# Queries and keys of five batches come in through DRAM rows and transposing DMAs in place of VectorE block transposes (sparse attention feeding a bilinear feed-forward layer)

## The chip, the cores and the metric

The kernel runs on one core of a Trainium2 chip. The core has a matrix engine (TensorE, PE in the profile, with its weight loads shown as PEld), VectorE (DVE), ScalarE (ACT), GpSimd (POOL) and a queue engine SyncE (SP), and 16 DMA engines that serve all queues. The metric is the device time of one execution in microseconds (us). Three runs of the kernel before took 330.50, 330.77 and 330.81 us; their median is 330.77.

## The reference

Eight batches of eight heads, 576 tokens, head width 64, all inputs float32. Heads 0 to 3 attend to the 32 latest tokens (local); heads 4 to 7 to earlier tokens with the same position modulo 32 (strided). The heads' outputs, side by side, are the 4608 x 512 input of a bilinear layer:

```python
scores = scale * np.matmul(q, k.transpose(0, 1, 3, 2))
mask_local = (rel >= 0) & (rel < stride)                      # stride = 32
mask_strided = (rel >= 0) & (pos[None, :] % stride == pos[:, None] % stride)
scores = np.where(masks[None], scores, -1e9)                  # heads 0-3 local, 4-7 strided
attn = softmax(scores);  x = (attn @ v) as rows of 512
return (x @ w_a) * (x @ w_b) @ w_out                          # 512 -> 1536 -> 512
```

## The kernel before, in words

**Stages.** Batch 0's attention runs by itself. After it the feed-forward layer runs over nine tiles of 512 tokens, and the attention of batches 1 to 7 is cut into small steps that are put between its matmuls. A tile has 16 slots: 12 `ffn_ab` (L627; eight 512-wide matmuls give both projections of 128 hidden units, ScalarE copies one out of PSUM, VectorE multiplies it with the other into `pf`) and 4 output slots (`ffn_y` L874 for tiles 0 and 1, `ffn_ys` L862 for tiles 2 to 8, which works with sums `ps` of pieces of `pf`, made by `fast_s` L753). Tiles 7 and 8 (`JOINT`) use the same kind of sums for the first projections: `wsum` of the weights (L656, L661) and `xsum` of the activations. Batch b's attention runs beside tile b-1, and tile b needs it.

**The order is written out by hand.** Every engine runs its instructions in program order. `do(i, fn, ...)` (L997) hangs a function behind slot i, where slot 16 t is the first of tile t; `LATER` (L587) and `IN_Y` (L590) place the attention steps of batches 3 to 7, counted from slot 16 (b-1): S0 to S7 are score units (`S_p` L379: matmuls; `S_x`: exponential on ScalarE; `S_m` L415: mask by a bitwise AND on VectorE), V0 to V7 value units, O0 and O1 store finished rows to DRAM (`rows_out` L505), I0 and I1 bring them back transposed into `xT` (`rows_in` L512). Two units make up one pair of heads, each with half of the pair's blocks. Before a slot's list is run, POOL copies one element of that slot's result (`pace`, L1060), so the DMAs that POOL issues follow the slots; SP has no such copy and goes on as soon as what its next DMA needs is there.

**q and k.** Scores need them with the head width on the partitions: `kT` for k, and for q a pair of buffers `qz` with zeros in the half that belongs to the other head of a pair, so that both heads of a pair go through one matmul. Batches 0 and 1 are transposed on PE. From batch 2 (`FIRST_D`) POOL's queue loads them, cast to bf16, into `kl`, `ql` (local, L213) and `natk`, `natq` (strided, L204), one DMA for each head. VectorE transposes 32x32 blocks (`step_D` L321; L328 four times and L333 six times for a batch), and SP copies the blocks to `kT` and `qz` (L343, L347), 24 copies a batch. There are two sets of buffers, for even and odd batches. `rezero` (L352) writes the zeros of one set on POOL at slot 14.

**Value units.** `step_VT` (L516), used for strided heads from batch 2, makes the value product with the head width on the partitions and the row sums beside it, takes 1/sum on ScalarE (Ln L536, Exp L537), and multiplies the two heads of a unit in two VectorE instructions into `xT` (L543).

**Weight sums.** `wsum_make` runs at slots 98 to 105, in tile 6: sums of `w_a` on VectorE, those of `w_b` on POOL, eight instructions each (L666).

Of the kernel before, what the change touches and what calls it, by code (L numbers as in the profile page):

```python
# [10 lines left out]
ALU = mybir.AluOpType  # L11
# [20 lines left out]
def kernel(  # L32
# [230 lines left out]

    held = {}
# [56 lines left out]
    def step_D(b, z, nm, part):  # L321
# [15 lines left out]
        if last:  # L337
            for nm, c in {"k": (("k", 0),), "q": (("q", 0), ("k", 1), ("q", 1))}[nm]:
# [10 lines left out]
                if (nm, c, z) == ("q", 0, 0) and b - 1 > FIRST_D:  # L349
                    rows_in(b - 1, 1)  # L350

    def rezero(b):  # L352

        for j in range(2):
            for t in qz_buf[b % 2][j]:
                nc.gpsimd.memset(t[32:64] if j == 0 else t[64:96], 0.0)
# [22 lines left out]
    def S_p(b, u):  # L379
# [136 lines left out]
    def step_VT(b, u):  # L516
# [70 lines left out]
    LATER = {-1: "S0", 0: "S1", 1: "V0", 2: "S2", 3: "V1 O0", 4: "S3", 5: "V2", 6: "S4 I0", 7: "V3 O1", 8: "S5", 9: "V4",  # L587
# [39 lines left out]
    def ffn_ab(t, f, mid, ab=None):  # L627
# [28 lines left out]
    wsum = [[h.rearrange("p (c g m) -> p c g m", c=2, g=FG) for h in homes] for homes in (  # L656
        [flat(vl_buf[0])[:, WS * z:WS * (z + 1)] for z in range(2)] + [flat(t)[:, :WS] for t in qz_pair[0]],
        [flat(vs_all[0])[:, WS * z:WS * (z + 1)] for z in range(2)] + [flat(nat_s[nm]) for nm in "qk"])]
    xsum = {t: flat(qz_pair[1][t - 7])[:, :8 * HT].rearrange("p (n c m) -> p n c m", n=4, c=2) for t in JOINT}

    def wsum_make(s, n, eng):  # L661
        w, s_ = (lambda e, j: wviews[s][:, j, :, :, e]), wsum[s]
        a, b, op = ((w(1, 0), w(1, 1), ALU.add), (s_[0], w(0, 0), ALU.subtract), (w(0, 0), w(1, 0), ALU.subtract),
                    (w(0, 1), s_[1], ALU.subtract))[n]
        for c in range(2):
            eng.tensor_tensor(s_[n][:, c], a[:, c], b[:, c], op=op)  # L666
# [33 lines left out]
    def joint(t):  # L700
# [3 lines left out]
        for half, (plain, *gs) in enumerate(JOINT[t]):  # L704
            banks = {x: eight(x) for x in "Ya Yb Xb Zb Xa Za".split()}
            order = JOINT_ORDER[half].split()
            for at_, (k, m) in enumerate(order):
# [10 lines left out]
                else:  # L718
# [190 lines left out]
    with tc.manual_schedule(engines={ENG.PE, ENG.SP, ENG.Pool, ENG.DVE, ENG.Activation}):  # L909
# [83 lines left out]
        steps[16 * (B - 2) + 9][-1][1].append("I1")  # L993
# [15 lines left out]
        for b in range(FIRST_D, B):  # L1009
# [13 lines left out]
            gs = {2: (14, 14, 15, 15, 16, 16, 17, 17, 18, 18), 3: (8, 9, 10, 11, 12, 13, 14, 15, 16, 17)}.get(b) or (  # L1023
                3, 5, 7, 9, 12, 13, 14, 15, 16, 17)
# [69 lines left out]
```

## Time and profile before

The profile is of one execution.

| | |
|---|---|
| median of three runs | 330.77 us (330.50 to 330.81) |
| the profiled execution | 331.63 us, its span 329.9 us |
| granted TensorE clock | 1.00 |
| busy share of the span | PE 96%, DVE 81%, ACT 57%, POOL 55% |
| block transposes on DVE from batch 2 on | L328 24 times (765 ns), L333 36 times (704 ns) |
| DVE multiply into xT (L543) | 48 times, 445 ns |
| weight sums (L666) | DVE 8 times, 543 to 553 ns; POOL 8 times, 1627 to 1952 ns |
| loads of q and k on POOL's queue, batches 2 to 7 | 96 DMAs, 72 or 96 KB each |
| copies to kT and qz on SP's queue | 144 DMAs |
| transposing DMAs xT from xd | 11, median 4.5 us from issue to landing |

The page's first part gives each engine's busy time, the second the span in 40 slices with the busy share in tenths. A line of a group or of a wait names the line of the kernel, the engine, and the tiles as output<-input. A window gives, for a stretch of the span, the busy time of each engine, and at its end the granted clock, the DMA share and GB/s. PE's matmuls are pipelined, so their listed lengths overlap.

### The profile page before, as it was taken

To read this page: it belongs to the slowest core of one execution; us is meant where nothing else is said; L and a number is where in the kernel's file an instruction comes from. 1 tells how busy PE (TensorE), PEld (TensorE's weight loads), DVE (VectorE), ACT (ScalarE), POOL (GpSimd) and SP (SyncE) were. 2 spreads that over 40 slices of the span, in tenths; PEclk is the share of its full clock that TensorE was granted. 3 is DMA by queue.
4 is the path that set the end of the run, shared out by engine and by line. 5 is a ranking of instruction groups with operands and counts; after the bars stand their busy time and mean duration, and the time that the engine had idled before them with its cause. 6 is when DMAs were issued, how large, how long until landed. Compare 5 with 4: busy or idle time off the path is not lost.

```text
span 329.9 us, 7496 instructions
## 1 busy us (share of the span) xinstructions
PE 317.1 (96%) x2691; PEld 212.8 (64%) x2720; DVE 267.3 (81%) x551; ACT 188.7 (57%) x320; POOL 180.2 (55%) x295
## 2 busy tenths in 40 slices
PE   8999999999999999999999999999986799999995
PEld 6754555445555586557999875578543577787775
DVE  7766887888778889889889888988999977864882
ACT  6764764468764575457644764476544555525532
POOL 8845836899857444754475347632278405312350
PEclk9999999999999999999999999999999999999999
DMA  9999999899999999999999999998164013003003
GB/s 158 149 204 201 203 182 168 185 182 130 141 211 130 135 100 92 124 208 121 119 120 215 123 114 107 188 171 103 31 173 59 0 24 108 0 0 129 2 1 127
DMA packets 111920, 40.73 MB, mean 123 GB/s; under 512 B 89868, under 2 KB 108940, under 8 KB 111884
## 3 DMA queue, kind: packets, MB, share of 16 engines
q0 software_dynamic: 85968, 19.48, 64.7%
q1 hardware_dynamic: 25772, 20.71, 26.0%
q8 instruction: 21, 0.34, 0.4%
q14 instruction: 15, 0.12, 0.1%
q10 hardware_dynamic: 144, 0.07, 0.1%
HBM read 39.51 MB, written 11.06 MB: 153 GB/s over the span
## 4 chain that ended last, share of the span: by engine, by line
PE 72%; DMA 8%; DVE 8%; POOL 7%; issue 3%; ACT 1%; POOLq 0%; DVEq 0%
PE mm L624 32%; PE mm L818 13%; PE mm L880 5%; DMA vl<-in_v_dram 4%; DMA shared<-in_q_dram 4%; PE st L389 3%; PE o L527 2%; PE eA L624 2%; PE eXb L728 2%; PE eXa L728 2%; PE eB L624 2%; DVE ps L760 2%; POOL shared L198 2%; PE eYa L818 2%; DVE pf L648 2%
## 5 line engine op out<-in xcount | busy, mean ns | idle before, releaser
L624 PE MATMUL mm<-xT,wb_sb 128*128 128x512 bf16 (+1 forms) x373 | 85.0, 352 | 4.2 <-DVE pf L648 3.9
L624 PE MATMUL mm<-xT,wa_sb 128*128 128x512 bf16 (+1 forms) x360 | 83.9, 351 | 0.7
L645 ACT COPY a_sb<-mm 128x512 f32<-128x512 f32 x82 | 47.9, 585 | 49.0 <-PE mm L624 41.5
L624 PEld LDWEIGHTS <-wb_sb 128*128 128x128 bf16 x416 | 40.1, 98 | 39.9 <-issue 5.2
L624 PEld LDWEIGHTS <-wa_sb 128*128 128x128 bf16 x416 | 37.3, 98 | 22.7 <-DVE xT L543 0.3
L1060 POOL CAST pace<-pf 1x1 f32<-1x1 bf16 x71 | 22.8, 321 | 45.2 <-DVE pf L648 31.8
L648 DVE TENSOR_TENSOR pf<-a_sb,mm 128x512 bf16<-128x512 f32 x60 | 40.7, 679 | 6.4 <-PE mm L624 6.1
L410 ACT ACTIVATE p<-st 72x576 bf16<-72x576 f32 (+1 forms) x56 | 36.4, 650 | 16.2 <-PE st L389 16.0
L543 DVE TENSOR_TENSOR xT<-o,xr 64x288 bf16<-64x288 f32 x48 | 21.4, 445 | 13.5 <-ACT xr L537 13.0
L818 PEld LDWEIGHTS <-ps 128*128 128x128 bf16 x288 | 27.9, 98 | 3.9 <-DVE ps L760 0.7
L732 POOL TENSOR_TENSOR pf<-vl 128x256 bf16<-128x256 f32 x12 | 8.7, 729 | 30.8 <-DVE vl L741 30.8
L536 ACT ACTIVATE xr<-o 64x576 f32<-64x576 f32 x28 | 18.1, 647 | 12.6 <-PE o L527 12.3
L880 PE MATMUL mm<-wo_sb,pf 128*128 128x512 bf16 x93 | 23.2, 379 | 0.2
L818 PEld LDWEIGHTS <-pf 128*128 128x128 bf16 x216 | 20.1, 98 | 3.7 <-DVE pf L648 1.2
L244 POOL DMA_DIRECT2D vs<-in_v_dram x24 | 19.6, 818 | 5.0 <-PE mm L818 2.4
L760 DVE TENSOR_TENSOR ps<-pf 128x512 bf16<-128x512 bf16 (+2 forms) x42 | 21.6, 514 | 0.6
L818 PE MATMUL mm<-wf,ps 128*128 128x256 bf16 x180 | 21.5, 273 | 0.5 <-DVE ps L760 0.5
L537 ACT ACTIVATE xr<-xr 64x576 f32<-64x576 f32 x28 | 19.1, 683 | 0.9
L213 POOL DMA_DIRECT2D ql<-in_q_dram x24 | 15.9, 664 | 6.2 <-DMA wo_sb<-in_moe_w_out_dram 4.6
L213 POOL DMA_DIRECT2D kl<-in_k_dram x24 | 16.1, 671 | 5.3 <-issue 3.2
L791 ACT COPY y_sb<-mm 128x512 f32<-128x512 f32 x20 | 11.7, 585 | 12.1 <-PE mm L818 10.5
L650 DVE TENSOR_TENSOR pf<-a_sb,mm 128x512 bf16<-128x512 f32 x22 | 14.9, 677 | 4.5 <-ACT a_sb L645 2.7
(242 smaller groups left out, 640.0 us busy)
## 6 DMA issues: line engine op xcount, KB each, us to landing
out_dram<-y_sb SPq DMA_DIRECT2D x12, 512.0 KB, 5.5
out_dram<-y_sb SPq DMA_DIRECT2D x11, 256.0 KB, 4.2
vl<-in_v_dram POOLq DMA_DIRECT2D x6, 384.0 KB, 7.7
kl<-in_k_dram POOLq DMA_DIRECT2D x24, 72.0 KB, 3.1
ql<-in_q_dram POOLq DMA_DIRECT2D x24, 72.0 KB, 3.3
vs<-in_v_dram POOLq DMA_DIRECT2D x24, 72.0 KB, 4.2
wo_sb<-in_moe_w_out_dram POOLq DMA_DIRECT2D x4, 384.0 KB, 9.8
natk<-in_k_dram POOLq DMA_DIRECT2D x20, 72.0 KB, 3.5
```

What stands on the lines that cost most here:

```text
L213: nc.gpsimd.dma_start(out=t[32 * h:32 * h + 32], in_=src[b, h].rearrange("(i y) d -> y i d", y=32))
L244: nc.gpsimd.dma_start(out=vs_buf[b % 2][:, h, :, 0:D], in_=v[b, HL + h].rearrange("(p r) d -> p r d", r=RS))
L410: nc.scalar.activation(p_flat(p)[:M, :2 * W].rearrange("p (i n) -> p i n", n=2 * n), st[:M].rearrange("p a (i n) -> p (a i) n", n=256)[:, ...
L537: nc.scalar.activation(r, r, ACT.Exp, scale=-1.0)
L543: nc.vector.tensor_mul(dst.rearrange("d (p r) -> d p r", r=RS)[:, :, G * half:G * (half + 1)], o[:64, j, :W].rearrange("d (g p) -> d p g", ...
L624: nc.tensor.matmul(ps_[:, c0:c0 + n], lhsT=w[:, kk, 128 * f:128 * (f + 1)], rhs=xT[:, kk, x0:x0 + n], start=(kk == first and c0 == 0), sto ...
L645: nc.scalar.copy(a_sb, ab[0])
L648: nc.vector.tensor_mul(pf[:, f, :].rearrange("p (i a s) -> p a i s", i=2, s=16), halves(a_sb), halves(ab[1]))
L760: nc.vector.tensor_tensor(s[:, n], a, b, op=op)
L818: nc.tensor.matmul(bank[b][:, q], lhsT=lhs(g, q), rhs=rhs(g), start=k in "172" and q == 0 and g == 0, stop=g == FG - 1, skip_group_check=True)
L880: nc.tensor.matmul(ybank[j], lhsT=pf[:, f, 128 * j:128 * (j + 1)], rhs=wo_sb[:, f], start=(f == 0), stop=(f == FD - 1))
L1060: nc.gpsimd.tensor_copy(pace, done)
```

## The change

For batches 3 to 7, six DMAs of POOL's queue (`rows_load`, at slots 2 to 7 of tile b-2) read q and k from DRAM in float32 and write them as bf16 rows to DRAM: k and two copies of q for the local heads, and the same for the strided heads. Each copy of q has room for both heads of a pair, and only one head's columns are written; the other columns were filled with zeros once (`rows_zero`, slot 17). Six transposing DMAs of SP's queue (`rows_take`, at slots 5, 6, 7, 9, 10, 11) bring the rows into `kT` and `qz`. The 32x32 transposes, the copies to `kT` and `qz`, and `rezero` go for these batches; batch 2 keeps them. Strided rows hold a head's 8 x 64 values in a row, so a strided unit becomes all 576 tokens of one head instead of half of two heads; `S_p` and `step_VT` have a branch for it, and the multiply into `xT` is one instruction. I1 gets a place of its own at slot 9. All weight sums go to VectorE, one 128x768 instruction at a slot: ten at every third slot of tiles 4 and 5 from slot 65 on, six at every second slot of tile 6 from slot 97 on, with new homes in memory.

```diff
+    def rows_zero(z):
+        rows["q", z] = [dram.tile([(S, NR)[z], (4, 8)[z] * D], BF16, tag=f"zq{z}{j}", name=f"zq{z}{j}", bufs=1) for j in range(2)]
+        rows["k", z] = dram.tile([(S, NR)[z], (4, 8)[z] * D], BF16, tag=f"zk{z}", name=f"zk{z}", bufs=1)
+        for j in range(2):
+            t = rows["q", z][j].rearrange("a b -> (a b)").rearrange("(p n m) -> p n m", p=64, n=2)
+            zero = qz_pair[1][0][64 - 64 * j:128 - 64 * j, j].rearrange("p c n -> p (c n)")
+            nc.sync.dma_start(out=t, in_=zero.unsqueeze(1).to_broadcast([64, 2, 2 * S]))
+
+    def rows_load(b, nm, z, j=0):
+        h0 = b * H + HL * z
+        src = {"k": k, "q": q}[nm].rearrange("b h s d -> (b h) s d")
+        if nm == "k":
+            if z:
+                nc.gpsimd.dma_start(out=rows["k", 1].rearrange("(h p) m -> h p m", h=HL),
+                                    in_=src[h0:h0 + HL].rearrange("h (p r) d -> h p (r d)", r=RS))
+            else:
+                nc.gpsimd.dma_start(out=rows["k", 0].rearrange("s (h d) -> h s d", d=D), in_=src[h0:h0 + HL])
+        elif z:
+            nc.gpsimd.dma_start(
+                out=rows["q", 1][j].rearrange("n (i e d) -> n i e d", e=2, d=D)[:, :, j],
+                in_=src[h0:h0 + HL].rearrange("h (p i e) d -> (h p) i e d", e=2, i=RS // 2)[:, :, j])
+        else:
+            nc.gpsimd.dma_start(out=rows["q", 0][j].rearrange("s (c e d) -> c s e d", e=2, d=D)[:, :, j],
+                                in_=src[h0:h0 + HL].rearrange("(c e) s d -> c s e d", e=2)[:, :, j])
+
+    def flat_s(t):
+        return t[:, :4 * NR].rearrange("p (i m) -> p i m", i=4)
+
+    def rows_take(b, nm, z, j=0):
+        if nm == "k":
+            t = kT_buf[b % 2][z]
+            nc.sync.dma_start_transpose(out=flat_s(t.rearrange("p c n -> p (c n)")) if z else t[:, :, PAD:], in_=rows["k", z])
+        else:
+            t = qz_pair[b % 2][z][:, j]
+            nc.sync.dma_start_transpose(out=flat_s(t.rearrange("p c n -> p (c n)")) if z else t, in_=rows["q", z][j])
...
-                if (nm, c, z) == ("q", 0, 0) and b - 1 > FIRST_D:
-                    rows_in(b - 1, 1)
-
-    def rezero(b):
-
-        for j in range(2):
-            for t in qz_buf[b % 2][j]:
-                nc.gpsimd.memset(t[32:64] if j == 0 else t[64:96], 0.0)
...
+            if b > FIRST_D and c >= 2:
+                kf = kT.rearrange("p c n -> p (c n)")
+                for i in range(G):
+                    k0 = i * NR + (u - HL) * NP
+                    nc.tensor.matmul(sv[:, i, :2 * n].rearrange("p (j n) -> p j n", j=2), lhsT=kf[:, k0:k0 + 128],
+                                     rhs=qz_pair[b % 2][1].rearrange("p j c n -> p j (c n)")[:, :, k0:k0 + n],
+                                     start=True, stop=True)
+                return
...
+        if b > FIRST_D and c >= 2:
+            by_token = lambda x: x[:, :, :W].rearrange("d j (g p) -> d p g j", p=NP)
+            r = r.rearrange("d (p g j) -> d p g j", g=G, j=2)
+            nc.scalar.activation(r, by_token(o[64:]), ACT.Ln)
+            nc.scalar.activation(r, r, ACT.Exp, scale=-1.0)
+            dst = xT[64 * half:64 * half + 64, c, S * (b % XR):S * (b % XR + 1)]
+            nc.vector.tensor_mul(dst.rearrange("d (p g j) -> d p g j", g=G, j=2), by_token(o[:64]), r)
+            return
...
-    LATER = {-1: "S0", 0: "S1", 1: "V0", 2: "S2", 3: "V1 O0", 4: "S3", 5: "V2", 6: "S4 I0", 7: "V3 O1", 8: "S5", 9: "V4",
+    LATER = {-1: "S0", 0: "S1", 1: "V0", 2: "S2", 3: "V1 O0", 4: "S3", 5: "V2", 6: "S4 I0", 7: "V3 O1", 8: "S5", 9: "V4 I1",
...
-    def wsum_make(s, n, eng):
...
-        for c in range(2):
-            eng.tensor_tensor(s_[n][:, c], a[:, c], b[:, c], op=op)
+    def wsum_make(s, n, c):
...
+        nc.vector.tensor_tensor(made(n), a, b, op=op)
...
+                for n, (nm, z, j) in enumerate((("k", 0, 0), ("q", 0, 0), ("q", 0, 1), ("k", 1, 0), ("q", 1, 0), ("q", 1, 1))):
+                    do(g0 + n + 2, rows_load, b, nm, z, j)
+                    do(g0 + n + (5, 5, 5, 6, 6, 6)[n], rows_take, b, nm, z, j)
                 for h in range(HL):
-                    do(g0 + h + (2 if b == FIRST_D + 1 else -2), load_qk, b, False, (h,))
-                    do(g0 + h + (6 if b == FIRST_D + 1 else 2), load_qk, b, True, (h,))
                     do(g0 + h + 10, load_vs, b, (h,))
...
-        for n in range(4):
-            do(16 * (NT - 3) + 2 * n + 2, wsum_make, 0, n, nc.vector)
-            do(16 * (NT - 3) + 2 * n + 3, wsum_make, 1, n, nc.gpsimd)
+        for n in range(16):
+            do(16 * (NT - 5) + 3 * n + 1 if n < 10 else 16 * (NT - 3) + 2 * (n - 10) + 1, wsum_make, n // 8, n // 2 % 4, n % 2)
...
-        do(14, rezero, 1)
         do(28, fill_v, vs_buf[1])
+        do(17, rows_zero, 0)
+        do(17, rows_zero, 1)
```

The sizes are D = 64, S = 576, HL = 4 heads, RS = 8 tokens in a strided row, NR = 288 strided rows, W = 288, NT = 9 tiles. In the text, k0 is the load or take of k for the local heads, q0 even and q0 odd are the two copies of q for them, and k1 and q1 those for the strided heads.

More of the change, by code (lines that the diff above doesn't have):

```diff
@@ L259, in load_wo @@
         )
+    rows = {}
+    NR = HL * S // RS
+    def rows_zero(z):
[30 more added lines that the diff above has]
+            nc.sync.dma_start_transpose(out=flat_s(t.rearrange("p c n -> p (c n)")) if z else t, in_=rows["q", z][j])
     held = {}
@@ L524, in step_VT @@
                     vt = vl_buf[b % 2][:, (2 * c + j) * 6 + 3 * half + i]
+                elif b > FIRST_D:
+                    vt = vs_buf[b % 2][:, u - HL, 2 * i + j]
                 else:
@@ L655, with wsum_home @@
     WS = 2 * FG * 128
-    wsum = [[h.rearrange("p (c g m) -> p c g m", c=2, g=FG) for h in homes] for homes in (
-        [flat(vl_buf[0])[:, WS * z:WS * (z + 1)] for z in range(2)] + [flat(t)[:, :WS] for t in qz_pair[0]],
-        [flat(vs_all[0])[:, WS * z:WS * (z + 1)] for z in range(2)] + [flat(nat_s[nm]) for nm in "qk"])]
-    xsum = {t: flat(qz_pair[1][t - 7])[:, :8 * HT].rearrange("p (n c m) -> p n c m", n=4, c=2) for t in JOINT}
-    def wsum_make(s, n, eng):
-        w, s_ = (lambda e, j: wviews[s][:, j, :, :, e]), wsum[s]
-        a, b, op = ((w(1, 0), w(1, 1), ALU.add), (s_[0], w(0, 0), ALU.subtract), (w(0, 0), w(1, 0), ALU.subtract),
-                    (w(0, 1), s_[1], ALU.subtract))[n]
-        for c in range(2):
-            eng.tensor_tensor(s_[n][:, c], a[:, c], b[:, c], op=op)
+    wsum = {}
+    def wsum_home(i):
+        if i < 3:
+            at_ = ([nat.tile([128, NY, D], BF16, tag=f"{nm}l", name=f"{nm}l") for nm in "kq"] if i == 0 else
+                   [blocks(nm, i - 1) for nm in "kq"])
+            at_ = [flat(t)[:, :WS // 2] for t in at_]
+        else:
+            at_ = (flat(nat_s["kq"[i - 3]]) if i < 5 else flat(vl_buf[0])[:, WS * (i - 5):WS * (i - 4)] if i < 7 else
+                   flat(qz_pair[0][0])[:, :WS])
+            at_ = [at_[:, WS // 2 * c:WS // 2 * (c + 1)] for c in range(2)]
+        return [t.rearrange("p (g m) -> p g m", g=FG) for t in at_]
+    xsum = {t: flat(qz_pair[1][t - 7])[:, :8 * HT].rearrange("p (n c m) -> p n c m", n=4, c=2) for t in JOINT}
+    def wsum_make(s, n, c):
+        if c == 0:
+            wsum[s, n] = wsum_home(4 * s + n)
+        w, made = (lambda e, j: wviews[s][:, j, c, :, e]), (lambda n: wsum[s, n][c])
+        a, b, op = ((lambda: (w(1, 0), w(1, 1), ALU.add)), (lambda: (made(0), w(0, 0), ALU.subtract)),
+                    (lambda: (w(0, 0), w(1, 0), ALU.subtract)), (lambda: (w(0, 1), made(1), ALU.subtract)))[n]()
+        nc.vector.tensor_tensor(made(n), a, b, op=op)
     def x_part(t, j, k):
@@ L725, in joint @@
                         for c in range(2):
-                            w = wsum[s][lhs][:, c, g] if isinstance(lhs, int) else wviews[s][:, lhs[1], c, g, lhs[0]]
+                            w = wsum[s, lhs][c][:, g] if isinstance(lhs, int) else wviews[s][:, lhs[1], c, g, lhs[0]]
                             x = xsum[t][:, rhs, c] if isinstance(rhs, int) else x_part(t, *rhs)[:, c]
@@ L992 @@
                     steps["y", b - 1, n] = [(b, names.split())]
-        steps[16 * (B - 2) + 9][-1][1].append("I1")
         at = {}
@@ L1017 @@
             else:
+                for n, (nm, z, j) in enumerate((("k", 0, 0), ("q", 0, 0), ("q", 0, 1), ("k", 1, 0), ("q", 1, 0), ("q", 1, 1))):
+                    do(g0 + n + 2, rows_load, b, nm, z, j)
+                    do(g0 + n + (5, 5, 5, 6, 6, 6)[n], rows_take, b, nm, z, j)
                 for h in range(HL):
-                    do(g0 + h + (2 if b == FIRST_D + 1 else -2), load_qk, b, False, (h,))
-                    do(g0 + h + (6 if b == FIRST_D + 1 else 2), load_qk, b, True, (h,))
                     do(g0 + h + 10, load_vs, b, (h,))
                 do(g0 + (10 if b == FIRST_D + 1 else 7), load_vl, b)
-            gs = {2: (14, 14, 15, 15, 16, 16, 17, 17, 18, 18), 3: (8, 9, 10, 11, 12, 13, 14, 15, 16, 17)}.get(b) or (
-                3, 5, 7, 9, 12, 13, 14, 15, 16, 17)
+                continue
+            gs = (14, 14, 15, 15, 16, 16, 17, 17, 18, 18)
             for (z, nm, part), g in zip(((0, "k", 0), (0, "k", 1), (0, "q", 0), (0, "q", 1), (1, "k", 0), (1, "k", 1),
```

## The prediction

> **What bounds the kernel now.** I read the page's first two parts first (where is TensorE not full?), then windows of time, then who waited, then the instructions of the one bad stretch.
>
> ```profile
> PE 317.1 (96%) x2691; PEld 212.8 (64%) x2720; DVE 267.3 (81%) x551; ACT 188.7 (57%) x320; POOL 180.2 (55%) x295
> ...
> PE   8999999999999999999999999999986799999995
> ...
> DVE  7766887888778889889889888988999977864882
> ...
> DMA  9999999899999999999999999998164013003003
> ```
>
> TensorE (PE) is full but for the ends and slices 29 to 31. Windows (PE, weight loads, DVE, ACT, POOL busy; clock; DMA share, which passes 1 when one engine has several packets in flight; GB/s):
>
> ```profile
> 80.00:120.00 40.00, 39.74 (x281) 21.83 (x285) 33.18 (x68) 26.22 (x43) 25.48 (x46) 1.00 1.13 142
> 200.00:240.00 40.00, 39.78 (x300) 24.60 (x303) 35.12 (x73) 23.31 (x39) 17.87 (x36) 1.00 0.89 121
> ...
> 240.00:250.00 10.00, 7.99 (x53) 3.92 (x53) 9.93 (x16) 3.74 (x7) 7.35 (x8) 1.00 0.73 152
> 250.00:255.00 5.00, 4.05 (x28) 1.94 (x27) 5.00 (x7) 2.95 (x5) 5.00 (x4) 1.00 0.29 59
> 255.00:260.00 5.00, 3.11 (x31) 2.15 (x31) 4.92 (x8) 2.17 (x4) 4.20 (x5) 1.00 0.00 0
> ```
>
> From 80 to 240 us, where the block transposes stand, the four windows of 40 us leave PE idle 0.26, 0.16, 0.16 and 0.22 us: 0.80 in all. VectorE (DVE) is 83 to 88% busy there and is waited for almost nowhere, so time taken off it there is worth nearly nothing. From 240 to 260 DVE is full (19.85 of 20) and PE loses 4.85. PE's waits name it:
>
> ```profile
> PE mm L624 <- DVE pf L648: 3.9, 4, 1.1
> PE mm L818 <- DVE pf L648: 0.9, 1, 0.9
> ...
> PE mm L818 <- DVE ps L760: 0.5, 1, 0.5
> ```
>
> All of these fall between 244 and 262 us and sum to 5.3 us. What fills DVE there (start, length, instruction), with POOL's timeline below it:
>
> ```profile
> 242.52 0.41 DVE L760 TENSOR_TENSOR ps<-pf 128x512 bf16<-128x512 bf16 x1
> 244.14 1.75 DVE L760 TENSOR_TENSOR ps<-pf 128x512 bf16<-128x512 bf16 x1
> 246.42 1.42 DVE L428 TENSOR_TENSOR p<-p,mask_s 72x576 int16<-72x576 int16 x1
> 259.78 0.44 DVE L428 TENSOR_TENSOR p<-p,mask_s 72x576 int16<-72x576 int16 x1
> ```
>
> ```profile
> 243.80 3.72 POOL L666 TENSOR_TENSOR vs<-vs,wb_sb 128x768 bf16<-128x768 bf16 x2
> 249.98 3.73 POOL L666 TENSOR_TENSOR natq<-wb_sb 128x768 bf16<-128x768 bf16 x2
> ```
>
> The same DVE instruction takes 0.4 us alone and 1.3 to 1.9 beside a weight sum on POOL. Seven are stretched so: L428 1.93, 1.42, 1.43 against 0.45, L760 1.75, 1.75, 1.32, 1.15 against 0.42, 7.7 us in excess. DVE is full because POOL's eight sums collide with it.
>
> **The change, part by part.**
>
> *Weight sums.* All sixteen go to DVE, ten of them 30 to 60 us earlier. POOL's eight (14.1 us) end, and with them the 7.7 us of stretching. DVE still makes six at 0.545 us between 238 and 262, as many as now. Of the 19.85 us in 240 to 260, some 7.5 go with the stretching and 0.5 with the joined products below; 11.9 us stand in the 15 us that the stretch then takes, 80%, under the 88% of 200 to 240 where PE hardly waits. So I take the whole 5.3 us. From below: if half the waits stay, 2.6. The ten early sums (5.5 us) go where DVE loses more than that; without that cover they would lie in the 12 to 17% of DVE time that is idle there.
>
> *Block transposes.* For five batches 4 x 765 ns and 6 x 704 ns go: 7.28 us each, 36.4 in all. By the 0.80 us of idle PE between 80 and 240 this is worth at most that; I take 0.2 us, since only the waits on DVE can shrink. What comes next is PE itself.
>
> *Products of the attention output.* Score and value matmuls keep number and shape. The strided half's two 64x288 multiplies (0.90 us a pair) become one of 64x576: by the fixed part and slope of 64x288 at 445 ns and 128x512 at 679, about 0.75. Twenty units, 3 us on DVE, worth 0. The two ScalarE passes (647 and 683 ns) keep their size and read the banks in another order; if they doubled, ScalarE would go from 58 to some 74% in 200 to 240: still 0.
>
> *POOL's queue.* Per batch eight issues at 0.67 and eight at 0.60 go (10.2 us), six come at 0.6 to 1.36 (the 384 KB load of v is the largest row): at most 8. Zero fills of 4.4 us go. Each issue stands behind a pace copy as now: 0.
>
> *SP's queue.* Per batch 24 copies at about 0.6 us (14.4) go; six transposes come. The 144 KB one of now issues in 1.2 us, so twice the size takes 1.2 to 2.4: 7 to 14. Four zero stores (2.4 us at 0.6) come ahead of batch 2's last qz0s copies: those were issued at 68.5 to 71.0, land 3.1 later and are read at 77.5, so 1.1 us is left. Cost 0; without that margin about 1 us, once.
>
> *DMA traffic.* Rows of these steps:
>
> ```profile
> vl<-in_v_dram POOLq DMA_DIRECT2D x6, 384.0 KB, 7.7
> kl<-in_k_dram POOLq DMA_DIRECT2D x24, 72.0 KB, 3.1
> ...
> xd<-xl SPq DMA_DIRECT2D x10, 144.0 KB, 4.8
> ...
> xT<-xd SPq DMA_TRANSPOSE x11, 4.5
> ```
>
> Per batch there were 4608 pieces of 128 B and 576 of 1 KB; now 6912 and 288. Queue 0's 85,968 packets took 64.7% of 16 engines' 329.9 us, 39.7 ns each: 2016 more pieces cost 5.0 us of all 16 engines. A 144 KB transpose shows a share of 0.68 in a window of 1 us, so six double ones 8.2; the 1024 rows copied now go (26.0% over 25,772 packets is 53 ns, 3.4 us). Net 9.8 us per 33 us tile, 0.3 on a share of 0.9 to 1.4; between 149 and 151 us it reached 2.3 with PE full. Not a limit by itself.
>
> *The new chain of waits.* Load, then transpose, then scores, and SP stands still at each transpose until its load has landed. Behind take k0 waits I0; behind takes q0 wait O1 and I1, whose reader is the next tile's first matmul. In tile 3 of the trace pace copies end slots 2, 3, 4 at 134.3, 136.3, 138.2, which is when the k0, q0 even and q0 odd loads would be issued; S0 needs their transposes at 161.2. At the speed of v's load (3072 pieces in 7.7 us) the three loads' 4608 pieces land 11.6 us after 134.3, and 1.7 later for a DRAM target (xd 4.8 against kl 3.1 for 576 pieces each): 147.6. The last transpose lands by 152 to 155 (4.5 to 7.4, the row's range). Some 6 to 9 us are left, so the cost is 0; this is the value I take, as the same cast of the same 256-byte pieces is the nearest row. The other end is the second rival's.
>
> Sum: 5.3 + 0.2 - 0 = 5.5 us off, of which I leave 0.2 for new small waits: 5.3. The profiled execution took 331.63 (span 329.9 and 1.7 around it) and would take 326.3; the median shown is 0.9 lower, 330.77, so I predict 325.5.
>
> **The rivals.**
>
> *1. Casts to DRAM go out on few engines and land late (slower).* Every load now has 128 or 72 rows of SBUF outermost; k0 has 4 heads outermost and each q0 2 pairs, so the pieces could be split over 4 and 2 DMA engines: 576 in a row on each. At 39.7 ns that is 22.9 us: q0 odd, moving from about 139, lands at 163.6 with the DRAM surcharge, its transpose at 168.1, and PE stands 6.9 us at S0. Five batches make 34 us: 360. In the window 149 to 150 the engines moved 153 GB/s, 9.6 each, or 13.4 ns a piece; then q0 odd lands at 148.4 and nothing waits. It begins to cost at 28 ns (161.2 less 139, 1.7 and 4.5 leaves 16.0 us for 576) and outweighs the 5.3 us at 30. Midway at 33 ns PE waits 3.0 us a batch: 340. For it: no load of the trace has so few outermost rows, and an average piece costs more than 28. Against: packets overlap at the shares above 1. The Trainium skill's page "DMA: Bandwidth & Descriptors", section "Why a DMA increments its semaphore by 16 and not by 1", states this rule: the engine count is the largest number up to 16 dividing both patterns' slowest dimension. By it k0 would run on 4 engines and each q0 on 2, and the sum would be this rival's; no transfer of the trace before shows such a shape.
>
> *2. The waits of 240 to 262 stay.* If DVE is held up there by its own order (mask, product, sum before pf), not by POOL, only the 0.2 and a part of the 5.3 come: 329. For it: six sums remain. Against: 7.7 us of stretching lie exactly beside POOL's sums.
>
> *3. It frees DVE and PE follows.* If PE were really paced by DVE's 83 to 88%, 36 us less would show as more than 5.3. Against: 0.80 us idle in 160. At most 324.7, with the 0.80 all gained.
>
> **How the numbers follow.** Forecast 0.58 (323.5 to 327.5); late casts 0.32, of which 0.26 slower, 0.03 the same, 0.03 still faster; waits stay 0.08 (0.05 faster, 0.01 the same, 0.02 slower); rival 3 0.02. Faster 0.68, the same 0.04, slower 0.28, the bound being 0.2%, about what a measurement of this kernel tells from no change. The range must reach into the late casts: 323.5 to 339 leaves out some 0.15, nearly all above.
>
> **What would show it.** Right: no L666 on POOL, L428 and L760 at 0.4 to 0.5 us throughout, PE over 99% from 240 to 256, no PE wait naming a transpose or xd. Wrong: S0 (L389) or the first matmul of a tile (L624) waiting for kT, qz or xT at each tile's start, SP standing at the transposes for over 10 us, loads landing after 15 us or more.

## The result, and the profile after

The changed kernel takes 465.9 us (median of four runs, 462.51 to 466.99) where the kernel before took 330.79 us beside it: 1.406 times as long (95% interval 1.398 to 1.414). The profiled execution took 466.99 us, its span 465.3. The prediction was 325.5 us, with a range to 339: wrong in sign and far outside. Medians and ratios below leave out runs more than 1.5% above the fastest run of the same kernel (the first experiment has 338.5 us so, and 341.07 over all its runs).

The page's busy shares, some rows of its 40 slices, and its line for POOL's DMA queue (packets, MB, share of 16 engines):

```profile
PE 328.0 (71%) x2691; PEld 217.1 (47%) x2720; DVE 232.1 (50%) x489; ACT 189.7 (41%) x320; POOL 155.4 (33%) x216
...
PE   8999996500999900999007992059950299999996
...
PEclk9999999765899955899757998569985599999999
...
q0 software_dynamic: 208128, 19.94, 62.2%
```

TensorE was full before; from the eighth slice on there is a hole in every tile, with all engines low together, and the granted clock falls there (0.50 from 350 to 365 us, inside the last long hole). No engine took over as the bound. The waits of PE (us in total, times, longest) name the transfers of the change:

```profile
PE st L428 <- DMA qz1l<-zq: 49.7, 2, 24.9
PE st L428 <- DMA qz0l<-zq: 45.9, 2, 24.0
PE o L568 <- DMA vs<-in_v_dram: 13.9, 1, 13.9
PE st L428 <- DMA qz0s<-tq: 9.0, 1, 9.0
PE o L568 <- issue: 8.0, 1, 8.0
```

Four waits of 21.9 to 24.9 us stand at S0 of batches 4 to 7, two at value units (13.9 for v, which comes through the same queue, and 8.0 for which the profile names no releaser), and one of 9.0 us in batch 2. With the small ones (xT 1.8, qz0l from tq 0.7, issue 0.7) that is 129.7 us. Take off the 5.3 us of waits for `pf` and `ps` that are gone, and add 10.9 us by which PE's busy time rose with the same 2691 matmuls (328.0 against 317.1, the lower clock): 135.3, and the spans differ by 135.4.

What happens in one tile is in POOL's timeline (start, length, instruction, and in brackets the idle time before it). L283 is the load of k0, L289 those of q0 even and odd, L280 and L285 those of the strided half:

```profile
136.69 2.98 POOL L283 DMA_DIRECT2D zk<-in_k_dram  x1 [0.76 <-issue]
...
149.62 2.94 POOL L289 DMA_DIRECT2D zq<-in_q_dram  x1 [9.78 <-DVE pf L697]
...
162.40 2.95 POOL L289 DMA_DIRECT2D zq<-in_q_dram  x1 [9.37 <-issue]
...
165.47 0.52 POOL L280 DMA_DIRECT2D zk<-in_k_dram  x1
...
166.10 0.82 POOL L285 DMA_DIRECT2D zq<-in_q_dram  x1
```

and SP's, in the same tile:

```profile
149.26 1.28 SPq L298 DMA_TRANSPOSE kT0l<-zk  x1
150.64 1.22 SPq L553 DMA_TRANSPOSE xT<-xd  x1
162.11 1.30 SPq L301 DMA_TRANSPOSE qz0l<-zq  x1
163.51 0.52 SPq L548 DMA_DIRECT2D xd<-xl  x1
175.39 2.19 SPq L301 DMA_TRANSPOSE qz0l<-zq  x1
```

Three casts go out one after the other, 12.9 and 12.8 us apart, and SP's takes follow each landing: 149.3, 162.1, 175.4. POOL issues the next cast 0.3 to 0.4 us after each take. In the next three tiles the two casts of q0 last as long (12.5 to 13.2 us from issue to take), k0 15.6 to 16.6. The last transpose lands at 184.5, PE having stood at S0 since 162.6. The strided casts and the loads of v come only behind the third cast. The DMA issues show the same (KB each, median us from issue to landing, over the local and the strided casts together); before, `vl` took 7.7 and `vs` 4.2:

```profile
zk<-in_k_dram POOLq DMA_DIRECT2D x10, 288.0 KB, 12.6
zq<-in_q_dram POOLq DMA_DIRECT2D x20, 144.0 KB, 12.6
...
vl<-in_v_dram POOLq DMA_DIRECT2D x6, 384.0 KB, 17.0
vs<-in_v_dram POOLq DMA_DIRECT2D x24, 72.0 KB, 14.4
```

The parts of the change that lie on the compute engines did what was said of them. A window over the tiles that hold the last attention and the early sums, which is free of loads (PE, weight loads, DVE, ACT, POOL busy; clock; DMA share; GB/s), and the joined multiply into `xT`:

```profile
380.00:440.00 60.00, 59.73 (x483) 44.05 (x487) 43.83 (x88) 33.28 (x59) 13.19 (x24) 1.00 0.19 55
```

```profile
L577 DVE TENSOR_TENSOR xT<-o,xr 64x576 bf16<-64x576 f32 x20 | 15.0, 750 | 19.8 <-ACT xr L575 19.6
```

**On how many engines a cast goes out** can be counted. POOL's queue carries 208,128 packets; with the rows put outermost in k0 and q0 (the first experiment, the same data) it carries 92,928. The 115,200 more hold 0.46 MB (19.94 against 19.48), 4 bytes each. They are 5 batches x 576 x (12 + 14 + 14): one packet of 4 bytes for each of the 576 pieces of an engine's row, on every engine that the cast does not use, if k0 is on 4 engines and each q0 on 2. With one q0 alone in the old form (E10) the surplus is 40,320 = 5 x 576 x 14, with both 80,640. The rule of the Trainium skill's page "DMA: Bandwidth & Descriptors", section "Why a DMA increments its semaphore by 16 and not by 1", the largest number up to 16 that divides both sides' slowest dimension, gives 4 and 2, and the trace agrees.

The first experiment also changes the order in which the pieces are written. The trace's records of single packets tell which of the two matters. While q0 even goes out alone (152.6 to 162.1 us), its 1152 packets of 128 bytes take 32.0 ns each, with 3.9 in flight in the mean; from 137 to 145 us of the first experiment such packets take 31.8 ns, with 12 in flight. A packet takes the same time in either order; fewer go at a time.

### The profile page after: what moved, and what is told of

The parts are those of the page before. It is cut to its first block, busy times and chain, and to the rows that moved or that the text cites. A ratio compares the mean times of both kernels' runs of the same rounds, so it can differ in the third digit from the quotient of the medians.

```text
span 465.3 us, 7147 instructions
## 1 busy us (share of the span) xinstructions
PE 328.0 (71%) x2691; PEld 217.1 (47%) x2720; DVE 232.1 (50%) x489; ACT 189.7 (41%) x320; POOL 155.4 (33%) x216
## 3 DMA queue, kind: packets, MB, share of 16 engines
q0 software_dynamic: 208128, 19.94, 62.2%
## 4 chain that ended last, share of the span: by engine, by line
PE 38%; DMA 29%; issue 23%; POOL 6%; SPq 2%; DVE 2%; ACT 0%; POOLq 0%; DVEq 0%
PE mm L673 19%; DMA zq<-in_q_dram 11%; DMA xT<-xd 7%; PE mm L940 3%; DMA vl<-in_v_dram 3%; DMA shared<-in_k_dram 3%; DMA vs<-in_v_dram 2%; PE mm L878 2%; PE eA L673 1%; DMA kT1l<-zk 1%; SPq L301 1%; PE eXb L788 1%; PE eXa L788 1%; PE eB L673 1%; POOL shared L198 1%
## 5 line engine op out<-in xcount | busy, mean ns | idle before, releaser
L289 POOL DMA_DIRECT2D zq<-in_q_dram x10 | 29.4, 2943 | 115.0 <-issue 48.6
L697 DVE TENSOR_TENSOR pf<-a_sb,mm 128x512 bf16<-128x512 f32 x60 | 41.1, 685 | 28.8 <-PE mm L673 15.4
L673 PEld LDWEIGHTS <-wa_sb 128*128 128x128 bf16 x416 | 38.7, 101 | 26.9 <-issue 4.9
L1120 POOL CAST pace<-pf 1x1 f32<-1x1 bf16 x64 | 14.5, 227 | 96.4 <-DVE pf L697 58.6
L428 PE MATMUL st<-qz1l,kT1l 128*128 128x192 bf16 x48 | 7.3, 265 | 49.7 <-DMA qz1l<-zq 49.7
L467 DVE TENSOR_TENSOR p<-p,mask_l 128x576 int16<-128x576 int16 x32 | 14.6, 455 | 52.4 <-ACT p L449 52.2
L428 PE MATMUL st<-qz0l,kT0l 128*128 128x192 bf16 x36 | 5.7, 273 | 46.5 <-DMA qz0l<-zq 45.9
L428 PEld LDWEIGHTS <-kT1l 128*128 128x128 bf16 x48 | 4.7, 104 | 52.7 <-issue 50.7
L428 PEld LDWEIGHTS <-kT0l 128*128 128x128 bf16 x36 | 3.5, 107 | 50.2 <-issue 48.5
L568 PE MATMUL o<-p,vs 72*128 72x72 bf16 x192 | 10.6, 198 | 21.9 <-DMA vs<-in_v_dram 13.9
L244 POOL DMA_DIRECT2D vs<-in_v_dram x24 | 19.9, 831 | 16.4 <-DMA zq<-in_q_dram 13.5
L577 DVE TENSOR_TENSOR xT<-o,xr 64x576 bf16<-64x576 f32 x20 | 15.0, 750 | 19.8 <-ACT xr L575 19.6
L568 PEld LDWEIGHTS <-vs 72*128 72x128 bf16 x192 | 9.5, 99 | 25.4 <-DMA vs<-in_v_dram 14.0
## 6 DMA issues: line engine op xcount, KB each, us to landing
zk<-in_k_dram POOLq DMA_DIRECT2D x10, 288.0 KB, 12.6
zq<-in_q_dram POOLq DMA_DIRECT2D x20, 144.0 KB, 12.6
vs<-in_v_dram POOLq DMA_DIRECT2D x24, 72.0 KB, 14.4
```

Of the source, the lines that this page charges most:

```text
L244: nc.gpsimd.dma_start(out=vs_buf[b % 2][:, h, :, 0:D], in_=v[b, HL + h].rearrange("(p r) d -> p r d", r=RS))
L289: nc.gpsimd.dma_start(out=rows["q", 0][j].rearrange("s (c e d) -> c s e d", e=2, d=D)[:, :, j], in_=src[h0:h0 + HL].rearrange("(c e) s d - ...
L467: nc.vector.tensor_tensor(pi, pi, mk, op=ALU.bitwise_and)
L577: nc.vector.tensor_mul(dst.rearrange("d (p g j) -> d p g j", g=G, j=2), by_token(o[:64]), r)
L673: nc.tensor.matmul(ps_[:, c0:c0 + n], lhsT=w[:, kk, 128 * f:128 * (f + 1)], rhs=xT[:, kk, x0:x0 + n], start=(kk == first and c0 == 0), sto ...
L697: nc.vector.tensor_mul(pf[:, f, :].rearrange("p (i a s) -> p a i s", i=2, s=16), halves(a_sb), halves(ab[1]))
```

## The experiments

The theory after the result: the three casts of the local half go out on few engines, last 12.6 us and more each and one after another, and all that stands behind them on POOL and SP is late. Rivals: the transposes and the added traffic would cost as much with any shape; or the time is lost only because the casts start too near to their readers.

**E1, rows outermost.** Both patterns of k0 and q0 are turned, the same bytes to the same places:

```diff
-                nc.gpsimd.dma_start(out=rows["k", 0].rearrange("s (h d) -> h s d", d=D), in_=src[h0:h0 + HL])
+                nc.gpsimd.dma_start(out=rows["k", 0].rearrange("s (h d) -> s h d", d=D),
+                                    in_=src[h0:h0 + HL].rearrange("h s d -> s h d"))
...
-            nc.gpsimd.dma_start(out=rows["q", 0][j].rearrange("s (c e d) -> c s e d", e=2, d=D)[:, :, j],
-                                in_=src[h0:h0 + HL].rearrange("(c e) s d -> c s e d", e=2)[:, :, j])
+            nc.gpsimd.dma_start(out=rows["q", 0][j].rearrange("s (c e d) -> s c e d", e=2, d=D)[:, :, j],
+                                in_=src[h0:h0 + HL].rearrange("(c e) s d -> s c e d", e=2)[:, :, j])
```

> The changed kernel with one thing altered: the casts k0 and q0 name the 576 rows as their outermost dimension, and the heads inside, on both sides. The same bytes go to the same places. Theory (few engines and a full queue): with 576 rows outermost each cast spreads over 16 engines, 144 or 72 pieces on each; POOL issues them in about 1.3 us or less without standing between them, they land within 8 us, no PE wait names zq or zk, and the time is what was predicted for the change, 325.5 (323.5 to 328). Rival A (casting 128-byte pieces to DRAM is slow by itself): the casts still land after 12 us and more and the time stays above 430. Rival B (the transposing DMAs from DRAM are the slow part, 6 to 10 us each): loads land early but S0 still waits; 335 to 400.

Measured: 338.5 us, 1.024 times before (1.017 to 1.030). 127 of the 135 us go with the order of the dimensions alone. In batches 4 to 7 POOL issues k0 in 1.64 and q0 in 1.32 to 1.36 us and stands for at most 0.7 us ahead of a cast; ahead of batch 3's first cast of q0 it stands 5.4 us, of which more below (E13). The casts land in 6.8 and 7.1 us, in the medians of their groups. What remains is 13.0 us above the prediction; the profiled execution (336.67 us, the shortest of four) waits so:

```profile
PE st L429 <- DMA qz1l<-zq: 3.6, 1, 3.6
PE mm L674 <- DMA xT<-xd: 3.6, 3, 1.4
PE o L569 <- DMA vs<-in_v_dram: 0.9, 1, 0.9
```

```profile
152.67 1.21 SPq L549 DMA_DIRECT2D xd<-xl  x1
153.98 4.94 SPq L302 DMA_TRANSPOSE qz1l<-zq  x1
162.35 1.16 SPq L554 DMA_TRANSPOSE xT<-xd  x1
```

O1's store goes out at 152.67, a take of q0 right behind it; I1, which waits for the store, follows 9.7 us later and the next tile's first matmul waits for it. From 140 to 160 us the DMA share is 1.78, against 1.38 before; over 140 to 200 it is 1.50 against 1.20. Transposes land 5.2 to 11.2 us after their issue in the medians of their groups, xT's among them 6.6 (4.5 before).

**E2 and E10, the few-engine casts one by one.** E2 turns k0 alone; E10 turns k0 and q0 even and leaves q0 odd:

```diff
+            o = "c s e d" if j else "s c e d"
...
+            nc.gpsimd.dma_start(out=rows["q", 0][j].rearrange(f"s (c e d) -> {o}", e=2, d=D)[:, :, j],
+                                in_=src[h0:h0 + HL].rearrange(f"(c e) s d -> {o}", e=2)[:, :, j])
```

> The changed kernel with only k0 turned to rows outermost; the two q0 casts keep 2 pairs outermost. Theory (a queue that has room for one such cast at a time): one of the three casts in series drops out, q0 even is issued at its slot, q0 odd some 12.6 us later when the even one is done; PE waits at S0 some 9 us a batch in place of 22, about 395 (380 to 410). If instead each cast were late by its own slowness and not by standing behind the one before, q0 odd would land as late as it does now and the time would stay at 450 or more.

> The changed kernel with k0 and q0 even rows first; q0 odd alone keeps its two outermost head pairs, so one cast a batch goes out on few engines. Three such casts a batch took 465.9 us, two 413, none 341.1. If each slow cast costs by itself (12.6 us from issue to landing, whatever goes before it), the costs stand at about 36 us a cast from none to two, and one gives 370 to 380. If they cost because they run one after another (POOL stands until the one before has room, so that the second starts 10 us late), the first is nearly free but for its own 5.5 us of later landing, and one gives 341 to 355, with an issue at its slot and no stand of POOL ahead of it.

Measured: 413.05 us (one run) and 380.06 us (ratio 1.151, 1.148 to 1.154). From none to three such casts a batch the kernel takes 338, 380, 413 and 466 us: 42, 33 and 53 us for each. So the theory that the first is nearly free and only the standing in line costs has fallen. With one of them POOL does not stand ahead of any cast of batches 4 to 7, and yet it costs 8.3 us a batch:

```profile
155.11 1.64 POOL L283 DMA_DIRECT2D zk<-in_k_dram  x1 [0.39 <-issue]
...
157.09 1.36 POOL L291 DMA_DIRECT2D zq<-in_q_dram  x1 [0.30 <-issue]
...
159.30 2.97 POOL L291 DMA_DIRECT2D zq<-in_q_dram  x1 [0.71 <-issue]
```

```profile
167.10 4.79 SPq L303 DMA_TRANSPOSE qz1l<-zq  x1
171.98 0.54 SPq L550 DMA_DIRECT2D xd<-xl  x1
179.24 1.28 SPq L303 DMA_TRANSPOSE qz1l<-zq  x1
181.49 1.16 SPq L555 DMA_TRANSPOSE xT<-xd  x1
```

The lone cast, issued at 159.30, can be taken at 179.24: 19.9 us, and 19.3 to 19.9 in the four tiles, where q0 in the series of three took 12.5 to 13.2. Over 576 pieces in a row that is 33 to 35 ns a piece against 23 at most. That its two engines carry the rest of the traffic as well is the likely reason, and is not shown. `vl` then lands in 22.7 us (14.4 in E1). The transpose behind the cast is slow too: S0 starts at 188.56, 9.3 us after the take. PE waits there for it in each of the four batches, 6.7 to 8.0 us:

```profile
PE st L430 <- DMA qz1l<-zq: 15.2, 2, 8.0
PE st L430 <- DMA qz0l<-zq: 14.2, 2, 7.5
```

From batch 4 on, POOL stands long ahead of a load only behind a few-engine cast, until SP begins to take that one: 9.0 to 13.7 us ahead of each q0 in the changed kernel, 12.2 to 14.9 ahead of q0 odd in E2. In E10 it stands 4.2 to 5.4 us ahead of the last two loads of v, and goes on at 179.53, 0.3 us after the take. The profile gives "issue" or an instruction long done as the cause of these stands, so that the queue has no room is inferred, not shown.

**E5, the same slow casts earlier.** For batches 4 to 7 k0, q0 even and q0 odd are loaded at slots -8, -2 and 4:

```diff
-                    do(g0 + n + 2, rows_load, b, nm, z, j)
+                    do(g0 + ((-8, -2, 4)[n] if n < 3 and b > FIRST_D + 1 else n + 2), rows_load, b, nm, z, j)
```

> The changed kernel (casts on 4 and 2 engines as it has them), with the k0, q0 even and q0 odd loads of batches 4 to 7 issued at slots -8, -2 and 4 of tile b-2 in place of 2, 3 and 4. Batch 3 stays as it is and keeps its loss (tile 1 ended at 128.8 us in place of 93.7). Theory: each cast by itself takes some 12.6 us and that is harmless; the harm is three of them in series behind one another just ahead of their reader. Spaced by 12 us and more, nothing stands: after tile 1 the tiles run as in the first experiment, 365 to 380 in all. Rival (few engines are slow enough by themselves, or their empty packets choke the other engines): 420 or more.

Measured: 430.6 us (one run). 35 of the 135 us go; the idea that the casts only start too late fell. A tile still lasts some 52 us, because the casts fill the queue:

```profile
204.79 2.93 POOL L289 DMA_DIRECT2D zq<-in_q_dram  x1 [10.54 <-DVE xT L577]
...
217.75 3.01 POOL L283 DMA_DIRECT2D zk<-in_k_dram  x1 [5.94 <-issue]
...
241.98 2.96 POOL L289 DMA_DIRECT2D zq<-in_q_dram  x1 [16.72 <-issue]
...
256.91 2.95 POOL L289 DMA_DIRECT2D zq<-in_q_dram  x1 [11.06 <-DVE pf L697]
```

k0 of 217.75 is taken at 241.86, q0 even at 256.53, q0 odd at 269.59, and POOL issues the next cast 0.1 to 0.4 us after each: 24.1, 14.6 and 12.7 us in a row, where a tile of before lasts 33. v's loads go out among them and land late (`vl` 18.5, `vs` 20.6 us to landing).

**E3 and E4, the weight sums by themselves.** E3 is the kernel before with POOL's eight sums on VectorE, at their old slots; E4 is E1 with the sums of `w_b` back on POOL:

```diff
-            do(16 * (NT - 3) + 2 * n + 3, wsum_make, 1, n, nc.gpsimd)
+            do(16 * (NT - 3) + 2 * n + 3, wsum_make, 1, n, nc.vector)
```

```diff
-        nc.vector.tensor_tensor(made(n), a, b, op=op)
+        (nc.gpsimd if s else nc.vector).tensor_tensor(made(n), a, b, op=op)
```

> The kernel before with the eight weight sums of POOL moved to VectorE at the same slots of tile 6, nothing else. Theory of the collision: 7.7 us of stretching leave VectorE, 8 x 0.545 = 4.4 us of sums come, so the full stretch of 240 to 262 shrinks by 3 us: 327.5 (326 to 329). Rival (VectorE is held up there by its own order and load): more work on it, 331 to 334.

> The first experiment's kernel with the eight sums of w_b back on POOL, at the slots that the change gave them (two in tile 5, six in tile 6). Theory of the collision: six POOL sums of 1.6 to 1.9 us in tile 6 stretch VectorE by some 5 us again, while VectorE sheds 3.3 us of sums and has no block transposes any more, so PE waits come back only in part: 1 to 2.5 us above the first experiment. If the block transposes' end is what gains and the sums are nothing, it takes the same time as the first experiment within 0.3 us.

Measured: E3 326.44 us, 0.987 times before (0.985 to 0.989), 4.2 us gained. What PE still waits for there, and its window from 240 to 260 us (PE busy 15.15 and POOL 16.55 before):

```profile
PE mm L818 <- DVE pf L648: 1.0, 1, 1.0
...
PE mm L624 <- DVE pf L648: 0.3, 1, 0.3
```

```profile
240.00:260.00 20.00, 18.68 (x153) 11.72 (x152) 18.87 (x43) 11.60 (x20) 5.99 (x8) 1.00 0.37 90
```

VectorE made sixteen sums there in place of eight and yet kept PE waiting 1.3 us in place of 5.3. From 239 to 258 us masks (L428) and sums of 128x512 (L760) take 0.41 to 0.45 us there. The stretching beside POOL's sums was the cause. E4 took 340.53 us (1.029, 1.023 to 1.034) and E1 338.5; the intervals overlap and single runs scatter over 3.5 us in E4 and 7 in E1, so this pair says nothing of the end time.

**E7 and E8, the transports by themselves.** The kernel before, with all its copies kept, and for batches 3 to 7 either the six transposing DMAs into spare tiles that nothing reads (E7), or the six casts, rows outermost, that nothing reads (E8):

```diff
+                for n, (nm, z, j) in enumerate((("k", 0, 0), ("q", 0, 0), ("q", 0, 1), ("k", 1, 0), ("q", 1, 0), ("q", 1, 1))):
+                    do(g0 + n + (5, 5, 5, 6, 6, 6)[n], rows_take, n, z)
```

```diff
+                    do(g0 + n + 2, rows_load, b, nm, z, j)
```

> The kernel before, unchanged, with six transposing DMAs a batch added for batches 3 to 7 at the slots of the change, from DRAM rows of zeros into a spare tile that nothing reads. Price of the transposes alone. Theory 1 (SP's order): they never wait for a load, so they only take SP's time, some 10 us a batch: 330.6 to 333. Theory 2 (crowded DMA engines, by the transposes): the kernel's own copies and transposes land later and PE waits: 335 or more.

> The kernel before, unchanged, with the six casts to DRAM a batch added for batches 3 to 7 (rows outermost, as in the first experiment), which nothing reads. Price of the casts alone, on top of the loads that the kernel has anyway. Theory 1: 330.6 to 333. Theory 2 (crowded DMA engines, by the casts' 128-byte pieces): 335 or more.

Measured: 368.21 us (1.115, 1.104 to 1.125) and 353.57 us (1.068, 1.063 to 1.074). Neither is free. Both carry the four zero stores at slot 17 as well, and of their cost a part is PE's wait for batch 2's last copies of q behind these stores (5.2 us in E7, before its first take goes out, and 4.2 in E8; none before). In E7 SP is what runs out: from 190.46 to 227.76 us copies, six takes and stores follow each other with 36.2 us of issuing in 37.3, more than a tile of before lasts; single takes hold it for 5.13 us (199.61) where the 144 KB transposes of xT hold it for 1.2 to 1.3. PE then waits for copies from `tq` and `tk` (8.7, 5.5 and 3.8 us). In E8 the casts crowd the others out of the DMA engines: POOL's queue has a share of 83.3% (64.7% before), and PE waits 8.2 us in three waits for xT, whose rows land in `xd` after 6.6 us (4.8 before).

**E6, E9, E11, E12, E13: E1 with the order of the queues changed.** E6 loads batches 4 to 7 at slots -4 to 1 and takes them at 0, 1, 2 and 10, 11, 12. The others change one or two more things in E6. E9: takes of the local half at slots 4, 5, 5 (behind O0 at 3), and the zero stores at slot 12 in place of 17. E12: those takes alone. E13: the zero stores at 12 alone. E11: as E9, but the zero stores at slot 5.

```diff
-                    do(g0 + n + 2, rows_load, b, nm, z, j)
-                    do(g0 + n + (5, 5, 5, 6, 6, 6)[n], rows_take, b, nm, z, j)
+                    early = b > FIRST_D + 1
+                    do(g0 + (n - 4 if early else n + 2), rows_load, b, nm, z, j)
+                    do(g0 + ((0, 1, 2, 10, 11, 12)[n] if early else n + (5, 5, 5, 6, 6, 6)[n]), rows_take, b, nm, z, j)
```

```diff
-        do(17, rows_zero, 0)
-        do(17, rows_zero, 1)
+        do(12, rows_zero, 0)
+        do(12, rows_zero, 1)
```

> The first experiment's kernel with the loads of batches 4 to 7 at slots -4 to 1 and the takes of the local heads at slots 0, 1, 2, those of the strided heads at 10, 11, 12, so that no take stands ahead of O0, I0, O1 or I1 on SP with a wait. Theory 1 (the first experiment's remaining 15 us come from SP's order: I1 and O1 behind takes that wait): they go, 325 to 329. Theory 2 (the 16 DMA engines are crowded, so that stores, transposes and v's loads all land later whatever the order): most of it stays, 334 to 342.

> The rows-first kernel with early loads, with SP's order changed at two places: for batches 4 to 7 the takes of k0 and both q0 come at slots 4 and 5, behind O0 (slot 3) and ahead of I0 (slot 6), in place of slots 0 to 2; and the zero stores of the copies of q come at slot 12 in place of 17. If what is left there (4.1 us at the first matmul of tile 3, with the lower granted clock behind it, some 6 us in all) comes from O0 standing behind takes whose casts have not landed (O0 issued at 116.75, behind takes of q0 from 110.20 on), O0 goes out some 10 us earlier and the kernel takes 325 to 328 us, at or below the 326.4 of the kernel before with its sums on VectorE. If it comes from the crowding of the DMA engines between 95 and 130 us (share 1.6 to 1.85), the first matmul of tile 3 waits as long as before, and the time stays at 332 to 336.

> The kernel with SP's order changed, with the zero stores of the copies of q at slot 5 in place of 12, where SP issued nothing until 40.8 us. There is one wait left of a transfer, 2.7 us at S0's second unit of batch 2 (qz0l, copied by SP at 60 to 65, beside the zero stores' traffic from 50 to 55). If the zero stores cause it, it goes and the kernel takes 324 to 325.5 us, below the 326.4 of the kernel before with its sums on VectorE. If the copies of batch 2 are late by the loads and stores that both kernels have there, the wait stays and so does the time, 326.5 to 328.

> The rows-first kernel with early loads and one edit alone: for batches 4 to 7 the takes of k0 and both q0 at slots 4 and 5, behind O0 and ahead of I0, in place of 0 to 2; the zero stores stay at slot 17. If the order of O0 and the takes was what cost the first matmul of tile 3 its 4.1 us, that wait goes here too, without the zero stores' move, and the copies of batch 2 wait 0.4 us as in the kernel with slots 0 to 2: 325.5 to 327.5 us. If the move of the zero stores made the difference, the wait stays and the kernel takes 331 to 334 us.

> The rows-first kernel with early loads and the other edit alone: the zero stores of the copies of q at slot 12 in place of 17, the takes of k0 and both q0 at slots 0 to 2 as before. With the stores at slot 17 POOL's first cast of q0 for batch 3 stood 5.7 us behind them, and all that follows on POOL and SP came later. If this head start of batch 3 is what the first matmul of tile 3 needs, its wait goes with this edit alone: 326.5 to 328 us. If O0's place ahead of the takes is needed as well, O0 goes out behind takes at about 115 as before and the wait of 4 to 6 us stays: 331 to 335 us.

| kernel | takes, batches 4 to 7 | zero stores | us | ratio to before (95% interval) |
|---|---|---|---|---|
| E1 | as in the change | 17 | 338.47 | 1.024 (1.017 to 1.030) |
| E6 | 0, 1, 2 | 17 | 334.01 | 1.009 (1.007 to 1.012) |
| E12 | 4, 5, 5 | 17 | 332.61 | 1.006 (1.003 to 1.009) |
| E13 | 0, 1, 2 | 12 | 327.70 | 0.991 (0.988 to 0.994) |
| E9 | 4, 5, 5 | 12 | 327.11 | 0.989 (0.988 to 0.991) |
| E11 | 4, 5, 5 | 5 | 328.44 | 0.994 (0.991 to 0.996) |

Moving loads and takes out of the crowd gives 4.5 us. In E6 every window from 140 to 280 us has PE full, and one wait above 1.1 us is left, at tile 3's first matmul, with the lower clock behind it:

```profile
PE mm L674 <- DMA xT<-xd: 4.1, 1, 4.1
```

```profile
125.00:130.00 5.00, 4.68 (x49) 4.01 (x47) 3.32 (x5) 3.17 (x6) 3.16 (x5) 1.00 1.85 159
130.00:135.00 5.00, 1.19 (x3) 0.41 (x3) 0.62 (x2) 0.40 (x1) 0.00 (x0) 0.73 1.13 154
135.00:140.00 5.00, 5.00 (x19) 2.19 (x18) 1.15 (x2) 1.82 (x3) 1.49 (x3) 0.59 1.30 170
```

I took O0's place behind the takes for its cause. E12 has that order put right and waits 5.9 us: that fell. E13 has the zero stores moved alone and the wait is gone. The zero stores at slot 17 (SP, 68.16 to 71.83 in E6) hold two things up: SP's copies of batch 2 and its takes of batch 3 behind them, and POOL, which stands 5.70 us before batch 3's first cast of q0 (73.48 in E6, 69.41 in E13). The lateness is handed on from batch 3's takes to the stores of tile 2, and grows: batch 3's first take goes out at 78.96 in E6 and at 77.06 in E13, I1 at 130.30 and at 121.53. Why it grows is not shown. In E13:

```profile
113.56 0.33 SPq L549 DMA_DIRECT2D xd<-xl  x1
117.62 1.18 SPq L554 DMA_TRANSPOSE xT<-xd  x1
118.91 0.52 SPq L549 DMA_DIRECT2D xd<-xl  x1
121.53 1.14 SPq L554 DMA_TRANSPOSE xT<-xd  x1
```

What E9 and E13 still lose is one wait of 2.7 and 2.9 us for batch 2's copies, issued among the zero stores' traffic. E11 has it at 0.8, but there the stores hold SP from 21.1 to 31.8 us and PE waits 2.2 us for first weights instead: nothing gained. The best of all these kernels is E3, with 326.44 us, none of whose transports are changed.

## Why the prediction was wrong, step by step

**Weight sums: right.** 5.3 us were forecast; E3 gained 4.2 with the sums at their old slots, leaving 1.3 of the waits. In E9, with the early slots as well, PE is busy for 19.95 of the 20 us from 240 to 260 (15.15 before), and no wait for `pf` is left above 0.2 us:

```profile
240.00:260.00 20.00, 19.95 (x158) 12.44 (x158) 17.23 (x36) 12.42 (x21) 3.16 (x10) 1.00 0.24 57
```

The second rival (the waits stay) has fallen: E3, with every block transpose in place, is as fast as E9, which has 36 us less of them.

**Block transposes: right,** worth next to nothing, and with that the third rival (PE follows DVE) has fallen. From 80 to 240 us VectorE is busy for 112.0 us in E9 and was for 138.4 before; PE is idle for 0.69 us there and was for 0.80. The window from 140 to 200 us, before and in E9:

```profile
140.00:200.00 60.00, 59.79 (x574) 48.09 (x574) 52.64 (x108) 36.68 (x60) 31.49 (x60) 1.00 1.20 144
140.00:200.00 60.00, 59.89 (x575) 48.25 (x575) 43.76 (x87) 36.81 (x61) 26.98 (x46) 1.00 1.47 161
```

**Products:** 750 ns, as worked out from the two rows.

**The new chain of waits: the step that failed,** in the sentence that took "the speed of v's load (3072 pieces in 7.7 us)" for the three casts and landed q0 odd at 147.6. v's load has 128 rows outermost, k0 four and q0 two; by the count of packets they went out on 4 and 2 engines. By that sentence q0 odd lands 13.3 us after the first issue (11.6 and 1.7); in the changed kernel it could be taken 38.7 us after (136.69 to 175.39), 25 us later than thought. The first rival had the engine counts, and named them as the cause. What it said against itself, that packets overlap, was true: a packet took 32.0 ns, a piece in a row at most 23. It did not help, because the three casts went one after another.

**The rival's price was mis-sized too.** It let three casts run side by side and asked what a piece costs, with harm from 28 ns on. A cast of q0 took at most 13.2 us in the changed kernel, 23 ns a piece, under that bound; by the rival's own sum nothing would have waited. Two things took it over the bound. Where three follow each other they ran in series, 38.7 us from the first issue to the last landing. Where one stood alone among other traffic, a piece cost 33 to 35 ns (E10); the rival's sum gives 3 to 4 us a batch for that, and PE waited 6.7 to 8.0, as the transpose behind the cast took 9.3 us and not the 4.5 of the sum. Hence 466 us, above even its 340 to 360.

**POOL's queue: "0" was wrong.** The issues were put at 0.6 to 1.36 us by their size; those of few-engine casts take 2.95, and POOL stands 9.0 to 13.7 us ahead of two of them in each tile from batch 4 on, with v's loads behind (13.9 us of PE's waits). With all engines in use the issues of k0 and q0 come near the row (1.32 to 1.64).

**DMA traffic and SP's queue: too cheap.** Even without few-engine casts 325.5 was missed by 13.0 us (E1). The rise of 0.3 of the share was right (1.50 against 1.20 from 140 to 200 us); that it limits nothing was wrong: stores and transposes land later in it (1.78 from 140 to 160), and the casts alone, with all engines in use, cost 23 us together with the zero stores (E8). The last transpose was to land in 4.5 to 7.4 us; groups' medians go to 11.2. "Behind takes q0 wait O1 and I1" was seen and priced at nothing because the casts were thought early enough. "1.1 us is left" for batch 2's copies did not hold: the four zero stores keep SP for 3.7 us (E6) to 4.6 (changed kernel) in place of 2.4, and PE waited for these copies 9.0 us in the changed kernel and 5.2 in E7, which has no casts. In E6 that wait is 0.3 us, and the zero stores still cost 6 us (E6 to E13) by holding up batch 3's casts and takes. With the order of the takes and the zero stores mended (E9), the forecast sum is met to within 1.6 us: 327.1 against 325.5.

## What to carry to other kernels

Before a load is given a new shape, look at the outermost dimension of both its sides: the nearest row of the profile by size and by piece is worth nothing if that row goes out on 16 engines and the new transfer on two or four. Price a queue's new work as a series first, its sum against the length of a tile, and side by side only where the trace shows that; then ask for each wait on an in-order queue what stands behind it, since an early small transfer (here four zero stores) can hand its lateness on for two tiles. And take a change of several parts apart: here the small part was worth all the gain, and the large one, at its best, nothing.

## What the runs showed of the hardware

- By the counts, a cast on k of 16 engines put a packet of 4 bytes on each of the other engines for every piece of a row: 115,200 in the changed kernel, where the whole queue needs 92,928 with all engines in use (E1).
- A few-engine cast is issued in 2.95 us where the same bytes on 16 engines take 1.32 to 1.64, and POOL issued a second one 0.1 to 0.4 us after SP began to take the first, having stood 9.0 to 14.9 us (changed kernel from batch 4 on, E2), which the profile shows as "issue" or as a releaser long done.
- In the window of a wait of 4.1 us of PE the granted clock was 0.73 and in the next 0.59 (E6); it was 0.59 over the 27 us from 160 to 187 around the wait of 21.9 us in the changed kernel; in all its busy time rose by 10.9 us. The Trainium skill's page "TensorE: Matmul & The Clock Gate", section "Part 1: The HAM clock gate", states that an idle window of about 3.4 us halves the clock; the wait of 4.1 us agrees, and beside the one of 2.7 us in E9 the clock stayed at 1.00.
- Transposing DMAs of 128 partitions by 1152 columns held SP for 1.3 to 5.1 us each, and landed in 3.4 to 11.2 us (medians of their groups in the changed kernel and E1).
